# Linear attention and feed-forward on one core: float16 numerators, six Strassen blocks of 256 tokens, block ends at batch ends, and a planner that models TensorE's clock

## The chip, the core and the metric

The kernel runs on one core of a Trainium2 chip. A core has a matrix engine (TensorE, in profiles PE, with its weight loads as PEld), a vector engine (VectorE, DVE), an activation engine (ScalarE, ACT), a general engine (GpSimd, POOL) and a queue for transfers (SyncE, SP), which work at the same time and wait for each other through semaphores. TensorE writes to PSUM, eight banks of 512 four-byte columns in each of 128 partitions; the other data lie in SBUF. The metric is the time of one execution on the device in microseconds (us); lower is better.

## The reference

```python
def _attn_ref(q, k, v, omega):                 # q, k, v: (8, 8, 576, 64), omega: (128, 64)
    m, D = omega.shape
    scale = 1.0 / np.sqrt(np.sqrt(D))
    q_s, k_s = (q * scale, k * scale)
    def phi(x):
        proj = np.einsum('bhsd,md->bhsm', x, omega)
        sq = np.sum(x * x, axis=-1, keepdims=True) / 2.0
        h = proj - sq
        h = h - np.max(h, axis=-1, keepdims=True)
        return np.exp(h) / np.sqrt(m)
    q_p, k_p = (phi(q_s), phi(k_s))
    kv = np.einsum('bhsm,bhsd->bhmd', k_p, v)
    z = np.sum(k_p, axis=2)
    num = np.einsum('bhsm,bhmd->bhsd', q_p, kv)
    den = np.einsum('bhsm,bhm->bhs', q_p, z)[..., None] + 1e-06
    return (num / den).astype(np.float32)

def _moe_ref(x, w_in, w_out):                  # x: (4608, 512), w_in: (512, 2048), w_out: (2048, 512)
    h = x @ w_in
    g = 0.5 * h * (1.0 + erf(h * np.float32(1.0 / np.sqrt(2.0))))
    return (g @ w_out).astype(np.float32)
```

The output of the attention, with its heads side by side, is x of the feed-forward part: 8 batches of 576 tokens are 4608 tokens of 512 numbers. The square term falls out with the maximum.

## The kernel before

**Units.** The attention is done in 32 units: a batch and a pair of heads, four to a batch. Units 0 to 7 (batches 0 and 1) are "plain": four-byte matmuls throughout (`unit_plain`). The other 24 are "split": a number is written as a high and a low part, and products are sums of the three products of parts that matter. A split unit (`split_pre`, `exps_op`, `split_post`) casts the loaded keys and queries (`x_high` on ACT, L776; `x_low` on POOL, L785) in five groups of keys (four of 256 columns, one of 128) and four groups of queries (288 columns each), and multiplies each with omega (`proj` L793, `proj_q` L815). DVE adds the parts and finds maxima (`proj_add` L803, `q_blocks` L818 and L820), the maxima are subtracted (`k_shift` on POOL L811, `q_shift` on DVE L844), ACT takes the exponential (L591). `k_high`, `k_low` (L886) and `v_a`, `v_b` (L878) split keys and values into float16 for `kv_split` (L897). The sums are copied to `kvz` and split into `kvh` and `kvl` (`kv_c` L915, `kv_d` L918), the queries are transposed back and split into `qh` and `ql` (`q_back` L851, `q_high` L854, `q_low` L857). These four are float32r, a four-byte type. `num` (L655) multiplies them, three matmuls of 288 columns for a half and a head; then come `den`, `rcp` and `div` (L666, L671 to L673, L704).

**Blocks.** The feed-forward part goes through the tokens in 13 blocks of `TBS`: 256, 256, ten of 384, and 256. Block 0 is done in four-byte numbers (`mm1` L1076, `mm2` L1102). The others are in float16 pairs, scaled by a power of two that comes from the maximum of the attention's output bound over all batches that the block touches (`chain`, L938, then `block_be`, `block_scales` L1055, `block_spread`). A block so waits for the last batch of which it holds a token.

Blocks 1 to 8 are plain: for each of 16 chunks of 128 hidden columns, twelve matmuls (4 parts of the depth x 3 products of parts) make h in PSUM (`mm1` L1081), ACT takes gelu (L1089) and the high part (`g_high` L1093), DVE the low part (`g_low` L1097), and each tile of 128 tokens takes three matmuls of 512 columns into its accumulator (`mm2`, L1105 to L1107).

Blocks 9 to 12, three of 384 tokens and one of 256, do the first layer by Strassen's method in Winograd's form: with tokens, depth and hidden columns each cut in two, seven products take the place of eight. POOL makes the sums of operands (`b_sum` L1254), ACT and DVE their parts (`b_high` L1260, `b_low` L1263). The products (`w_prod` L1294) of `GP` = 2 chunk pairs at a time go into three PSUM buffers U, V and W of GP x half the tokens columns; a copy (`w_seed`, `w_snap`, L1301 and L1304) or a sum (`c_sum` L1307) hands them on between products, and gelu, high and low follow for four quarters (L1319, L1325, L1328). The second layer is as in plain blocks (`w_mm2`, L1392 to L1394). The very last tile is stored in two halves of 256 columns (`cuts`; `store` L1114, `store_dma` L1117).

**Order.** No loop sets the order. The program first lists all operations with what they read, write and allocate (`op`); then the class `Planner` makes one list by simulating the engines: whenever an engine is free it takes the ready operation with the earliest due time. Costs are written beside each operation. Due times come from its successors' due times and from fitted numbers: `STARTS` for blocks, `UDUE` for halves of units, `OFF` for each function's name, bonuses in `X`. Each engine then executes its own list in this order. PSUM is handed out in three rings: `at` (3 buffers), `h` (2), `acc` (3).

Of the kernel before, what the change touches and what calls it, by code (L numbers as in the profile page):

```python
# [8 lines left out]
F32 = mybir.dt.float32  # L9
# [54 lines left out]
class Planner:  # L64
# [45 lines left out]
    def run(self, lat, hop, alloc, put):  # L110
# [117 lines left out]
def favor_attention_ffn(ctx: ExitStack, tc: tile.TileContext, qT, kT, v, omT, w_in, w_out, out):  # L228
# [7 lines left out]
    TB = TBS  # L236
# [51 lines left out]
    pair_at = [xsb[:, 0:2 * T], xsb[:, 2 * T:4 * T], flat0[:, VO:VO + 2 * T], flat0[:, VO + 2 * T:VO + 4 * T], xaf[:, 0:2 * T], xaf[:, 2 * T:4 * T]]  # L288
    pair_at += [w32f[:, 1, c:c + 2].rearrange("p c w -> p (c w)")[:, 0:2 * T] for c in (0, NF // 2)]
    pair_at = [t.rearrange("p (j t) -> p j t", j=2) for t in pair_at]  # L290
    tx_at = [flat0[:, VO + (4 + i) * T:VO + (5 + i) * T] for i in range(3)] + [xaf[:, 4 * T:5 * T]]
# [10 lines left out]
                vsc=2, bs=4, be=2, tx=X['tx'], ss=X['ss'], raw=2, r=2 if X['xm'] else 3, lo=2, qt=2, ql=2 if X['qm'] else 4, kvh=1, kvl=1, xh=X['xh'], xl=X['xh'], gh=X['gh'], gl=X['gh'], o=2)  # L302
    for k, b in bufs.items():
# [3 lines left out]
                 dt=(P, HS), rt=(P, HS), rc=(P, HS // 32), mx=(P, 4 * QB), nq=(P, 4 * QB), mc=(D, 4 * QB), kvs=(P, 2, D),  # L307
                 vsc=(P, 2), bs=(P, 6), be=(32, 1), raw=(P, 2048), r=(P, 2 * HS if X['xm'] else HS), lo=(P, 2, M), qt=(P, QW, HS), ql=(P, QW, HS),
                 kvh=(P, 2, P), kvl=(P, 2, P), xh=(P, T), xl=(P, T), gh=(P, 2 * T), gl=(P, 2 * T), o=(P, DM))
    kinds = dict(raw=I32, r=F32R, ql=F32R, kvh=F32R, kvl=F32R, xh=F16, xl=F16, gh=F16, gl=F16)  # L310
    pools = dict(raw=dp, r=late, lo=late, qt=late, ql=late, kvh=late, kvl=late, xh=mp, xl=mp, gh=mp, gl=mp, o=mp)

    def alloc(name, k):
        if name in ('at', 'h', 'acc'):
            G[k] = pp.tile([P, 512], F32, tag=name, name=name, bufs=bufs[name])
            return
# [9 lines left out]
        dt = F32R if name == 'qh' and k[1].split else kinds.get(name, F32)  # L326
# [80 lines left out]
    def w_lo(pc):  # L407
        nc.scalar.activation(pc.l or raw(pc)[1], raw(pc)[1].bitcast(U32), AF.Copy, scale=2.0 ** -29)
# [78 lines left out]
    def weights_in(win, i):  # L487
# [4 lines left out]
        op('ACT', 1.08, w_lo, pc, r=[rk], w=pc.lk if pc.l is not None else [rk + ('lo',)])  # L492
# [1037 lines left out]
```

## Time and profile before

| | |
|---|---|
| time, median of 3 runs | 984.11 us (983.89 to 985.91) |
| the profiled execution | 984.64 us |
| its span, first to last instruction | 982.9 us |
| mean granted TensorE clock | 0.993 |
| read from HBM, written | 60.36 MB, 9.44 MB |

The span is what the trace shows; the rest of an execution's time lies around it. A busy TensorE is not TensorE at its peak: matmuls overlap, each record lasts longer than its share of the stream, and its end is modelled. The distance between matmuls is therefore read from runs of them. "Idle before" and "waits" give the time in which an engine did nothing, and the instruction that released it. The granted clock is the share of its full clock that TensorE had in a stretch.

### The profile page before, as it was taken

Reading aid. Unit: us, or ns where it says so; the run is one execution under the profiler, and the core shown is the slowest. Engines: PE = TensorE matmul, PEld = TensorE weight load, DVE = VectorE, ACT = ScalarE, POOL = GpSimd, SP = SyncE. Lnnn points to the kernel's source line nnn. Section 1 sums busy time; section 2 is a strip of 40 time slices with the busy share of each in tenths; the row PEclk is TensorE's granted clock in tenths of the full one; section 3 lists DMA queues with packets and bytes.
Section 4 is the critical chain, followed back from the end, with each engine's and each line's share of the span. In section 5 each row is a group of like instructions: output and inputs, shape, how many; then the busy total and the mean of one; then the engine's idle time right before and its main releaser. Section 6 shows DMA issues by size and latency. Waiting matters only on the chain.

```text
span 982.9 us, 18957 instructions
## 1 busy us (share of the span) xinstructions
PE 951.7 (97%) x6572; PEld 625.3 (64%) x6572; DVE 768.7 (78%) x2023; ACT 764.7 (78%) x1591; POOL 419.5 (43%) x612
## 2 busy tenths in 40 slices
PE   7988999899999999999999999999999999999998
PEld 5765666656655555565656665665666777767776
DVE  4898998999989997898889986996989575642322
ACT  6998768799899879979799987787779675654453
POOL 2235345666647674752564533552565011220000
PEclk7999999999999999999999999999999999999999
DMA  9774324222213221322213222231111000000000
GB/s 270 219 230 143 131 57 128 63 83 63 63 55 89 76 62 58 82 67 83 62 38 102 66 52 70 62 90 43 50 49 49 10 2 33 2 22 12 1 34 22
DMA packets 46287, 71.01 MB, mean 72 GB/s; under 512 B 13680, under 2 KB 22256, under 8 KB 46192
## 3 DMA queue, kind: packets, MB, share of 16 engines
q1 hardware_dynamic: 46192, 69.81, 24.1%
q8 instruction: 52, 0.85, 0.4%
q14 instruction: 43, 0.35, 0.1%
HBM read 60.36 MB, written 9.44 MB: 71 GB/s over the span
## 4 chain that ended last, share of the span: by engine, by line
PE 68%; DVE 18%; ACT 5%; POOL 3%; issue 2%; DMA 1%; SPq 1%; ACTq 0%; POOLq 0%
PE h L1081 16%; PE h L1294 5%; PE acc L1105 5%; PE acc L1107 5%; PE acc L1106 5%; PE at L1294 5%; PE acc L1393 4%; PE acc L1394 4%; PE acc L1392 4%; PE acc L1102 3%; PE at L655 3%; PE h L1076 2%; DVE gl L1097 2%; PE at L793 2%; PE at L897 2%
## 5 line engine op out<-in xcount | busy, mean ns | idle before, releaser
L785 POOL TENSOR_TENSOR r<-xt,r 64x288 fp32r<-64x288 f32 (+2 forms) x216 | 178.2, 843 | 147.0 <-ACT r L776 107.1
L1081 PE MATMUL h<-xh,wih 128*128 128x384 f16 (+1 forms) x512 | 163.7, 320 | 8.3 <-DVE gl L1097 7.6
L1081 PE MATMUL h<-xl,wih 128*128 128x384 f16 (+1 forms) x512 | 163.7, 320 | 0.0
L1081 PE MATMUL h<-xh,wil 128*128 128x384 f16 (+1 forms) x512 | 163.7, 320 | 0.0
L1105 PE MATMUL acc<-woh,gh 128*128 128x512 f16 x368 | 140.2, 381 | 0.0
L1107 PE MATMUL acc<-wol,gh 128*128 128x512 f16 x368 | 139.5, 379 | 0.0
L1106 PE MATMUL acc<-woh,gl 128*128 128x512 f16 x368 | 139.5, 379 | 0.0
L1081 PEld LDWEIGHTS <-wih 128*128 128x128 f16 x1024 | 97.6, 98 | 55.2 <-issue 0.2
L1097 DVE SCALAR_TENSOR_TENSOR gl<-h,bs,gh 128x384 f16<-128x384 f32 (+1 forms) x128 | 75.6, 590 | 24.9 <-ACT gh L1093 23.5
L776 ACT CAST r<-xt 128x256 fp32r<-128x256 f32 (+2 forms) x216 | 82.2, 407 | 15.6 <-PE at L815 6.8
L1089 ACT ACTIVATE h<-h,bs 128x384 f32<-128x384 f32 (+1 forms) x128 | 69.0, 540 | 25.3 <-PE h L1081 23.9
L1093 ACT ACTIVATE gh<-h,bs 128x384 f16<-128x384 f32 (+1 forms) x128 | 72.3, 566 | 13.1 <-PE acc L1107 9.8
L1081 PEld LDWEIGHTS <-wil 128*128 128x128 f16 x512 | 50.0, 98 | 39.2 <-issue 11.8
L1393 PE MATMUL acc<-woh,gl 128*128 128x512 f16 (+1 forms) x192 | 69.4, 361 | 0.1
L1392 PE MATMUL acc<-woh,gh 128*128 128x512 f16 (+1 forms) x192 | 69.4, 362 | 0.0
L1394 PE MATMUL acc<-wol,gh 128*128 128x512 f16 (+1 forms) x192 | 69.4, 361 | 0.0
L1294 PEld LDWEIGHTS <-w 128*128 128x128 f16 x768 | 60.3, 98 | 11.1 <-issue 0.9
L1107 PEld LDWEIGHTS <-gh 128*128 128x128 f16 x368 | 36.0, 98 | 43.4
L793 PE MATMUL at<-om,r 128*128 128x256 f32 x216 | 53.6, 337 | 2.6 <-POOL r L785 2.0
L1105 PEld LDWEIGHTS <-gh 128*128 128x128 f16 x368 | 35.8, 97 | 31.6 <-issue 0.2
L417 POOL TENSOR_TENSOR w<-w 128x1024 int32<-128x1024 int32 x12 | 28.5, 2375 | 61.9 <-DVE w L414 35.3
L1106 PEld LDWEIGHTS <-gl 128*128 128x128 f16 x368 | 36.1, 98 | 27.2 <-issue 0.3
(285 smaller groups left out, 2549.8 us busy)
## 6 DMA issues: line engine op xcount, KB each, us to landing
xt<-in_kT SPq DMA_DIRECT2D x56, 288.0 KB, 3.9
xt<-in_qT SPq DMA_DIRECT2D x56, 288.0 KB, 3.8
out_x<-o SPq DMA_DIRECT2D x35, 256.0 KB, 2.1
raw<-in_w_in SPq DMA_DIRECT2D x16, 512.0 KB, 5.5
raw<-in_w_out SPq DMA_DIRECT2D x16, 512.0 KB, 4.4
w<-in_v SPq DMA_DIRECT2D x24, 320.0 KB, 3.0
vt<-in_v SPq DMA_DIRECT2D x8, 320.0 KB, 4.7
out_x<-o SPq DMA_DIRECT2D x2, 128.0 KB, 1.7
```

The lines of the kernel that those rows point to most:

```text
L776: nc.scalar.copy(G['r', u, x][:, 0:b - a], xf[:, a:b])
L785: nc.gpsimd.tensor_tensor(r, xf[D:, a:b], r, op=ALU.subtract)
L793: nc.tensor.matmul(o[:, t], r[:, t * P:(t + 1) * P], om, start=True, stop=True)
L1081: nc.tensor.matmul(h[:, 0:t], w, (G['xh', n, j], G['xh', n, j], G['xl', n, j])[k][:, 0:t], start=(i == 0), stop=(i == 3 * NJ - 1))
L1097: nc.vector.scalar_tensor_tensor(G['gl', n, c][:, 0:t], G['h', n, c][:, 0:t], G['bs', n][:, 3:4], G['gh', n, c][:, 0:t], op0=ALU.mult, op1 ...
L1105: nc.tensor.matmul(acc, gh[:, s], woh[:, c, c0:c1], start=(c == 0), stop=False)
L1106: nc.tensor.matmul(acc, gl[:, s], woh[:, c, c0:c1], start=False, stop=False)
L1107: nc.tensor.matmul(acc, gh[:, s], wol[:, c, c0:c1], start=False, stop=(c == NF - 1))
L1294: nc.tensor.matmul(b[:, g * h:(g + 1) * h], w, x[:, kt], start=first and k == 0, stop=last and k == 6 * GP - 1, skip_group_check=True)
L1392: nc.tensor.matmul(acc, gh, woh[:, c, c0:c1], start=begin, stop=False)
L1393: nc.tensor.matmul(acc, gl, woh[:, c, c0:c1], start=False, stop=False)
L1394: nc.tensor.matmul(acc, gh, wol[:, c, c0:c1], start=False, stop=end)
```

## The change

**Float16 numerators.** `kvh`, `kvl`, `qh`, `ql` become float16. So that they fit, queries are scaled by 2^15 and sums by 2^-22, and `den` takes the scale back (a third column of `vsc`). `q_low` and `kv_d`, subtractions, become a scaling and a subtraction in one instruction.

**Query groups.** Queries of a split unit go through projection, casts and maxima in three groups of 384 columns for four of 288.

**Blocks.** 256, 256, then 384, 256 and five of 384, then six of 256, which are the Strassen blocks: 1536 tokens for 1408. There are 15 blocks for 13, and Strassen still starts at block 9, at token 3072 for 3200. The ends at 1152 and 2304 are ends of a batch of 576. A Strassen group is four chunk pairs for two, so that U, V, W and the quarters are 512 columns wide; a quarter has a float16 buffer of its own (six for three of 768 columns); U comes from the ring `at` alone, W from `h` or `at`. Before the first Strassen block, `prime` writes each buffer of the ring `h` in full width with one matmul. The second layer takes quarters in the order 11, 22, 12, 21; quarter 21 is tile 0. The places of x in SBUF are assigned anew.

**The planner.** It follows TensorE's busy share in windows of 3.4133 us and doubles the cost of matmuls from a window under 0.6 on, until two windows over 0.95 have passed. Many operations' costs are other numbers (`w_sign` 1.14 for 1.21, `block_scales` 1.95 for 1.2), `STARTS`, `UDUE`, `OFF` and `X` are fitted anew, and a new table `MOVES` gives thousands of single operations an offset of their own.

Branches of other settings, unused before and after (`w_lo_p`, `w_high_p`, the split units with four-byte sums), come or go with it.

```diff
-TBS = (256, 256) + (384,) * 10 + (256,)
-X = dict(fb=1875.39, fbp=-594.94, ..., n0=9, h=2, at=3, vs=5, wr=('h', 'at'), tx=4, ss=4, xh=8, gh=3,
+NSC = 2.0 ** -22
+CLK0 = 2.9
+CLKW = 3.4133
+X = dict(fb=59.68, fbp=-1804.0, ..., tb=(384, 256, 384, 384, 384, 384, 384), h=2, at=3, vs=5, wr=(('h', 'at'),
+         'at'), gh=6, n32=1, xp=0, qs=0, wl=0, wg=0, r=3, lag=6)
+MOVES = {0: 73.7, 1: -37.5, 3: -94.1, ...
...
-            o.due += OFF.get(o.fn.__name__, 0.0)
+            o.due += OFF.get(o.fn.__name__, 0.0) + MOVES.get(o.id, 0.0)
...
+        seen, slow, good, wins = 0, False, 0, [0.0] * 1000
+        def clock(t, c):
+            nonlocal seen, slow, good
+            while CLK0 + (seen + 1) * CLKW <= t:
+                u = wins[seen] / CLKW
+                if not slow:
+                    slow, good = seen > 0 and u < 0.6, 0
+                else:
+                    good += u > 0.95
+                    slow = good < 2
+                seen += 1
+            if slow:
+                c *= 2
...
+                if o.e == 'PE':
+                    c = clock(t, c)
...
-    TB = TBS
+    KP = len(X['tb'])
+    N0 = 2 + KP
+    TB = (256, 256) + X['tb']
+    TB += (256,) * ((NTOK - sum(TB)) // 256)
...
-    QB = HS // 32
+    QG = 3
+    QS = R2 // QG
+    QB = QS // 32
...
-    kinds = dict(raw=I32, r=F32R, ql=F32R, kvh=F32R, kvl=F32R, xh=F16, xl=F16, gh=F16, gl=F16)
+    kinds = dict(raw=I32, r=F32R, ql=F16, kvh=F16, kvl=F16, gh=F16, gl=F16)
...
+        if name == 'qh' and k[1].split:
+            G[k] = G[k].bitcast(F16)[:, 0:R2]
...
     def q_high(u, g):
-        nc.scalar.copy(qv(G['qh', u], g), G['qt', u, g])
+        nc.scalar.activation(qv(G['qh', u], g), G['qt', u, g], AF.Copy, scale=KSC)
     def q_low(u, g):
-        nc.vector.tensor_tensor(G['ql', u, g], G['qt', u, g], qv(G['qh', u], g), op=ALU.subtract)
+        nc.vector.scalar_tensor_tensor(G['ql', u, g], G['qt', u, g], KSC, qv(G['qh', u], g), op0=ALU.mult, op1=ALU.subtract)
...
     def kv_c(u):
-        nc.scalar.copy(G['kvh', u], G['kvz', u])
+        nc.scalar.activation(G['kvh', u], G['kvz', u], AF.Copy, scale=NSC)
     def kv_d(u):
-        nc.vector.tensor_tensor(G['kvl', u], G['kvz', u], G['kvh', u], op=ALU.subtract)
+        nc.vector.scalar_tensor_tensor(G['kvl', u], G['kvz', u], NSC, G['kvh', u], op0=ALU.mult, op1=ALU.subtract)
...
-    GP = 2
+    GP = 4
+    NQ = NF // 2 // GP
...
     def wino_second(n, q):
-        NI, h = TB[n] // P, TB[n] // 2
-        order = ((0, 0), (1, 2), (1, 0), (1, 1), (0, 1), (0, 2)) if NI == 3 else ((0, 0), (1, 0), (1, 1), (0, 1))
...
+        for x, part in enumerate((11, 22, 12, 21)):
+            i = part % 10 - 1
             for g in range(GP):
...
+    def prime(i):
+        nc.tensor.matmul(G['prime', i], wih[:, 0, 0:P], woh[:, 0], start=True, stop=True)
...
-        if n == X['n0']:
+        if n == N0:
...
+            for i in range(X['h']):
+                seq('m1', 'PE', 0.25, prime, i, r=[('wh', 1, 0), ('wh', 0, 0)], new=[('h', ('prime', i))], due=when(n, 0), kind='P')
```

More of the change, by code (lines that the diff above doesn't have):

```diff
@@ L491, in weights_in @@
         op('ACT', 1.08, w_hi, pc, w=[rk + ('hi',)], r=[rk])
-        op('ACT', 1.08, w_lo, pc, r=[rk], w=pc.lk if pc.l is not None else [rk + ('lo',)])
+        on = X['wl'] >> (i + 8 * (1 - win)) & 1
+        op('POOL' if on else 'ACT', 1.36 if on else 1.08, w_lo_p if on else w_lo, pc, r=[rk], w=pc.lk if pc.l is not None else [rk + ('lo',)])
         op('DVE', 0.64, w_shift, pc, r=[rk, rk + ('hi',)], w=bk)
@@ L619, in bound_a @@
     def bound_a(u):
-        nc.scalar.activation(G['zr', u], sums(u)[1], AF.Copy, bias=TINY)
+        if u.split:
+            nc.scalar.activation(G['zr', u], sums(u)[1], AF.Copy, bias=TINY, scale=G['vsc', u.b][:, 2:3])
+        else:
+            nc.scalar.activation(G['zr', u], sums(u)[1], AF.Copy, bias=TINY)
     def bound_b(u):
@@ L692, in x_pair, with free_region @@
     def x_pair(n, a):
-        return pair_at[pair_of(n, a)]
+        kind, r, i = pair_of(n, a)
+        w = 2 * (T if kind == 'x' else TH)
+        return (regions[3][:, i, 0:w] if r == 3 else regions[r][:, i * w:(i + 1) * w]).rearrange("p (j t) -> p j t", j=2)
+    def free_region(r):
+        ks = [('xp', 'w', r, i, j) for i in range(4) for j in range(2)]
+        assert not any(k in PL.last for k in ks)
+        op(None, 0, nothing, w=ks + [('xp', 'x', r, a, j) for a in range(2) for j in range(2)] + (['xaf'] if r == 2 else []))
     def div(u, half):
@@ new lines, in split_post @@
+        op('ACT', 0.74, v_a, u, r=[u.vk, ('vsc', u.b), 'p2'], w=['vb'])
+        op('DVE', 0.85, v_b, u, r=[u.vk, ('vsc', u.b)], w=['vb'])
+        for g in range(len(KG)):
+            es = [('et', u.eb, t) for t in KG[g]]
+            n = len(KG[g])
+            op('POOL', 0.1 + 0.15 * n, k_high, u, g, r=es + ['kk'], w=[('kk', g)])
+            op('DVE', 0.07 + 0.135 * n, k_low, u, g, r=es, w=[('kk', g)])
+        for g in range(len(KG)):
+            op('PE', 0.088 * len(KG[g]), kv_split, u, g, r=['vb', ('kk', g)], w=[] if g == 0 else [pk],
+               new=[('at', pk), ('kvs', ('kvs', u)), ('kvz', ('kvz', u))] if g == 0 else [])
@@ L1035, in split_post @@
+        op('ACT', 0.2, kv_a, u, r=[pk], w=[('kvs', u)])
+        op('DVE', 0.2, kv_b, u, r=[pk, ('kvs', u)], w=[('kvz', u)])
+        op('ACT', 0.39, kv_b2, u, r=[pk], w=[('kvz', u)])
+        op('ACT', 0.31, kv_c, u, r=[('kvz', u)], new=[('kvh', ('kvh', u))])
+        op('DVE', 0.34, kv_d, u, r=[('kvz', u), ('kvh', u)], new=[('kvl', ('kvl', u))])
+        bound(u, ('kvz', u))
         for x, g in enumerate((0, 1) if X['qm'] else (0, 2, 1, 3)):
             c = 0.3 * X['qm']
-            op('DVE', 0.42 + c, q_back, u, g, r=[('eq', u.eb, y) for y in ((g, g + 2) if X['qm'] else (g,))], new=[('qt', ('qt', u, g))])
+            op('DVE', 0.42 + c, q_back, u, g, r=[('eq', u.eb, y) for y in range(QG)], new=[('qt', ('qt', u, g))])
@@ L1484, in favor_attention_ffn @@
         if n == 1:
-            op(None, 0, nothing, w=['xaf'] + [('xa', m, j) for m in range(2) for j in range(NJ)] + [('xp', k, j) for k in (4, 5) for j in range(2)])
+            op(None, 0, nothing, w=['xaf'] + [('xa', m, j) for m in range(2) for j in range(NJ)] + [('xp', 'x', 2, a, j) for a in range(2) for j in range(2)])
+        if 1 <= n < N0:
+            r = 2 if n == 1 else PLACE[n - 2]
+            if r < 3 and r not in PLACE[max(0, n - 1):]:
+                free_region(r)
     lat = dict(PE=0.18, ACT=0.107, DVE=0.07, POOL=0.046)
```

322 lines of the change are left out of this document (151 added, 171 removed), and 374 rows, old and new, of tables (MOVES, UDUE).

## The prediction

> **What bounds the kernel now.** I read the page first, then busy time by stage, then who waited for whom, then single groups. The page:
>
> ```profile
> span 982.9 us, 18957 instructions
> PE 951.7 (97%) x6572; PEld 625.3 (64%) x6572; DVE 768.7 (78%) x2023; ACT 764.7 (78%) x1591; POOL 419.5 (43%) x612
> ...
> PEclk7999999999999999999999999999999999999999
> ...
> PE 68%; DVE 18%; ACT 5%; POOL 3%; issue 2%; DMA 1%; SPq 1%; ACTq 0%; POOLq 0%
> ```
>
> TensorE is busy 97% of the span and holds 68% of the chain that ended last; VectorE holds 18%. A change is therefore worth the TensorE time that it removes, plus the TensorE idle time that it closes. The same by stage (length, then busy time of PE, PEld, DVE, ACT, POOL, granted clock, DMA share, GB/s):
>
> ```profile
> 0.00:14.00 14.00, 8.19 (x87) 6.50 (x88) 7.20 (x21) 6.78 (x16) 0.70 (x6) 1.00 0.86 258
> 14.00:24.20 10.20, 9.33 (x49) 7.88 (x50) 4.43 (x9) 8.50 (x24) 4.91 (x3) 0.50 1.05 283
> 24.20:78.80 54.60, 46.59 (x383) 34.27 (x380) 49.80 (x117) 49.93 (x105) 19.10 (x12) 1.00 0.70 217
> 78.80:82.20 3.40, 3.40 (x6) 1.34 (x5) 3.14 (x5) 2.94 (x5) 2.83 (x8) 0.50 0.27 111
> ...
> 150.00:350.00 200.00, 191.78 (x1197) 120.00 (x1196) 188.56 (x510) 175.02 (x382) 130.26 (x189) 1.00 0.26 74
> 350.00:740.00 390.00, 386.14 (x2372) 235.16 (x2371) 331.99 (x974) 324.56 (x693) 200.62 (x317) 1.00 0.24 66
> 740.00:930.00 190.00, 188.98 (x1569) 137.10 (x1569) 107.25 (x239) 119.22 (x228) 34.18 (x58) 1.00 0.04 15
> ```
>
> Four kinds of stage. Up to 78.8 us TensorE idles 5.8 + 0.9 + 8.0 = 14.7 us, while DMA is near full until 24 us and DVE and ACT are each about 91% busy after it. From 78.8 to 82.2 us it is busy all the time, but at a clock of 0.50: half of 3.4 us, 1.7 us, is lost. From 150 to 350 us DVE is 94% busy and TensorE idles 8.2 us. From 350 to 740 us it idles 3.9 us, and in the Strassen stage from 740 to 930 us only 1.0 us. In the window 150 to 360 us its two largest waits (total, times, longest) are:
>
> ```profile
> PE h L1081 <- DVE gl L1097: 5.7, 8, 1.7
> PE at L793 <- POOL r L785: 1.8, 1, 1.8
> ```
>
> First-layer products wait for a PSUM buffer that DVE's `g_low` (L1097) still reads. DVE, not TensorE, ends last there.
>
> **The Strassen blocks.** Two stretches of nothing but Strassen products (L1294; 60 matmuls of 192 columns, 24 of 128), then two of nothing but plain first-layer products (L1081; 24 of 256 columns, 24 of 384), and the mean of one Strassen matmul:
>
> ```profile
> 882.74:887.87 5.13, 5.11 (x60) 1.00 0.17 64
> 942.24:943.76 1.52, 1.50 (x24) 1.00 0.44 173
> ...
> 179.50:182.31 2.81, 2.79 (x24) 1.00 0.02 6
> 283.62:287.71 4.09, 4.08 (x24) 1.00 0.02 4
> ...
> L1294 PE MATMUL at<-xl,w 128*128 128x192 f16 x112 | 27.6, 246 | 0.0
> L1294 PE MATMUL at<-xl,w 128*128 128x128 f16 x48 | 8.6, 219 | 0.0
> ```
>
> A matmul's own 246 or 219 ns overlaps the next one's, so a run of n lasts one of these and n-1 intervals: (5.11-0.246)/59 = 82.4 ns for 192 columns, (1.50-0.219)/23 = 55.7 ns for 128. By its code a Strassen block has 7 products x 8 chunk pairs x 2 x 3 = 336 matmuls of half its tokens. Before: three blocks of 384 and one of 256, 1008 x 82.4 + 336 x 55.7 = 101.8 us. After: 2016 x 55.7 = 112.3 us, so **+10.5 us**. In exchange block 3 shrinks from 384 to 256 tokens: 192 plain matmuls, eight runs of 24 that are each 4.08-2.79 = 1.29 us shorter, **-10.3 us**. The second layer is the same number of matmuls. The 128 more tokens under Strassen are paid back by the shorter matmuls: **+0.2 us**, nothing. I give it ±1 us, the reading error of the runs.
>
> The groups are now four chunk pairs, 512 columns instead of 384. Their ACT and DVE steps (gelu, high, low, sums) become fewer and longer, and the casts of the operands more (7 x 6 for 7 x 4). I cost them at nothing: from 740 to 930 us DVE is busy 107 of 190 us and ACT 119. If that cover were gone, TensorE would wait where a product needs a sum read out of its bank. The copy (min, median, max) and the sum in question, of 256 and 384 columns:
>
> ```profile
> L1304 ACT COPY h<-h x10: 357/463/478, 746.9 to 965.6; 128x384 f32<-128x384 f32 x8, 128x256 f32<-128x256 f32 x2
> L1307 DVE TENSOR_TENSOR at<-h,wih x5: 432/566/566, 749.8 to 949.1; 128x384 f32<-128x384 f32 x4, 128x256 f32<-128x256 f32 x1
> ```
>
> For 512 columns that extrapolates to 570 and 700 ns, under a product between of 24 x 55.7 = 1340 ns; before it was 463 and 566 under 12 x 82.4 = 990. The margin grows from 0.42 to 0.64 us, so below nothing is excluded on TensorE, and the bound above is 12 groups x 3 handoffs x 0.7 = 25 us with no margin at all; I take 0. `prime` adds two matmuls of 512 columns:
>
> ```profile
> L1105 PE MATMUL acc<-woh,gh 128*128 128x512 f16 x368 | 140.2, 381 | 0.0
> ```
>
> At most 2 x 0.38, by the overlap seen above about half: **+0.4 us**.
>
> **Float16 numerators.** Two of the `num` matmuls (L655, 288 columns of four-byte operands), the first and the last of five in a row:
>
> ```profile
> 277.10 0.30 PE L655 MATMUL at<-qh,kvl 128*128 128x288 f32 x1
> ...
> 277.63 0.29 PE L655 MATMUL at<-ql,kvh 128*128 128x288 f32 x1
> ```
>
> Four intervals in 0.53 us, 132.5 ns each. In float16 288 columns lie between 2.79/24 and 4.08/24, less the overlapped end: 109.6 + 32/128 x 53.4 = 123 ns. There are 24 split units x 2 halves x 6 = 288: **-2.7 us**. The bounds are 0, if the operands' type doesn't matter, and -5, if the switches between types cost as much again. On DVE the lows (L857, L918) change from a subtraction to a scale and subtraction, and the query projection goes in 3 groups of 384 for 4 of 288:
>
> ```profile
> L818 DVE STREAM_TRANSPOSE et<-at 128x288 f32<-128x288 f32 x52 | 24.7, 474 | 0.8 <-PE at L815 0.5
> L820 DVE TENSOR_REDUCE mx<-et 128x9 f32<-128x288 f32 x52 | 23.6, 453 | 1.8
> L851 DVE STREAM_TRANSPOSE qt<-et 128x576 f32<-128x576 f32 x26 | 19.6, 761 | 2.9 <-ACT et L591 2.8
> L857 DVE TENSOR_TENSOR ql<-qt,qh 128x576 fp32r<-128x576 f32 x48 | 38.5, 812 | 3.2 <-ACT qh L854 3.1
> L878 DVE SCALAR_TENSOR_TENSOR vb<-w,vsc,vb 128x640 f16<-128x640 f32 x24 | 21.9, 914 | 0.0
> L1097 DVE SCALAR_TENSOR_TENSOR gl<-h,bs,gh 128x384 f16<-128x384 f32 x112 | 68.0, 607 | 24.2 <-ACT gh L1093 23.0
> ```
>
> A transpose costs (761-474)/288 = 1.0 ns per element, so 570 for 384; the reduce, with the same slope, 549. Per unit 4 x 927 = 3.71 becomes 3 x 1119 = 3.36 us. The new low of 576 lies between 607 and 914, at 837: +25 ns, twice per unit, and as much again for the low of the sums (L918), +0.1 at most. DVE loses about 0.25 us per unit, 6 us of its 769; POOL and ACT lose one of nine casts and subtractions per unit. None of it is on TensorE; it matters where DVE ends last.
>
> **Block ends and the order.** Block 3 was tokens 896 to 1280 and needed batch 2, the first with the long split attention. Its scale and the stall around its start:
>
> ```profile
> 267.14 0.14 DVE L938 TENSOR_REDUCE vexp<-cg 32x1 f32<-32x4 f32 x1
> ...
> 270.58 0.26 POOL L1055 TENSOR_SCALAR bs<-bs,wsc 32x1 f32<-32x1 f32 x1
> ...
> 275.06 0.50 PE L793 MATMUL at<-om,r 128*128 128x256 f32 x2 [1.79 <-POOL r L785]
> ```
>
> Batch 2's maximum came at 267.1 us, the scale at 270.6, and block 3's first matmul stands at 283.62 us (the window above): TensorE reached the boundary as soon as the data did. After, block 3 is 896 to 1152 and needs batch 1 alone. That is 192 x 0.109 + 96 x 0.216 (as 128 columns more take 53 ns more, 512 take 109.6 + 2 x 53.4) = 41.7 us of TensorE work which no longer waits for batch 2, in the very stage where DVE is late. With DVE's saving and freely moved due times I take both waits above as gone, **-7.5 us** of the 8.2 us idle there. Bounds: nothing (the order is fixed for each engine's queue, and a `gl` queued behind an attention step is late as before), and all idle after 150 us, 8.2 + 3.9 + 1.0 = 13.1 us.
>
> The planner now counts TensorE's windows of 3.4133 us and doubles its costs when it expects half clock. It can only move work so that the idle before 78.8 us doesn't trigger the slow window: **-1.7 us**, bounds 0 and 14.7 + 1.7. It takes 1.7 because TensorE stands in the way there, as the chain of waits in this stretch shows (start, length, link):
>
> ```profile
> 78.12 5.40 PE acc L1102 x8
> ```
>
> These are second-layer products of block 0, and nothing else ends later.
>
> **The end.** The last block of before splits its last tile in two column halves. After, parts come in the order 11, 22, 12, 21, so tile 0 ends last, and the halves are tile 1's. The last tile's store (two halves of 256, against one of 512) and its DMA:
>
> ```profile
> L1114 ACT ACTIVATE o<-acc,bs 128x512 f32<-128x512 f32 x4 | 2.7, 687 | 5.4 <-PE acc L1394 5.4
> L1114 ACT ACTIVATE o<-acc,bs 128x256 f32<-128x256 f32 x2 | 0.8, 472 | 1.6 <-PE acc L1394 1.6
> ...
> out_x<-o SPq DMA_DIRECT2D x35, 256.0 KB, 2.1
> ...
> out_x<-o SPq DMA_DIRECT2D x2, 128.0 KB, 1.7
> ```
>
> 687-472 ns and 2.1-1.7 us: **+0.6 us**.
>
> **The sum** is made against the profiled execution, 984.64 us with a span of 982.9, 0.05% over the median of 984.11. 984.6 + 0.2 + 0.4 - 2.7 - 7.5 - 1.7 + 0.6 = 973.9: I forecast **974 us**.
>
> **The rivals.**
>
> *Only the work changes (20%).* Waits are moved, not removed: 984.6 - 2.7 + 0.2 + 0.4 + 0.6 = 983.1 us with the slow window, 981.4 without. For it: DVE is 94% busy from 150 to 350 us and loses only 0.25 us per unit. This is also the case in which the change doesn't do what it says: Strassen's larger share is worth 0.2 us either way. A difference under 0.2%, 982.1 to 986.1 us, is about what a measurement of this kernel can't tell from none; I give 11 of the 20 to it and 9 to below.
>
> *The start is rearranged too (17%).* Half of the 14.7 us idle up to 78.8 us goes: 974 - 7.3 = 966.7 us. For it: all due times change. Against it: DMA, then DVE and ACT, are full there, and no work of theirs is removed.
>
> *`g_low` later than before (12%), slower.* One new order for all queues, in a stage with 6% of DVE free. Over the whole span the waits for `gl` are:
>
> ```profile
> PE h L1081 <- DVE gl L1097: 7.6, 10, 1.7
> ```
>
> Ten late ones, of 128. Each one queued behind one more attention step, such as L857's 0.81 us, is late by as much. With 20 late the wait doubles, and nothing else is won: 983.1 + 7.6 = 990.7 us. It decides from 3.0 us more waiting, four more late ones.
>
> *Short matmuls wait for their weights (2%), slower.* The weight load of one Strassen matmul:
>
> ```profile
> L1294 PEld LDWEIGHTS <-w x768: 95/98/101, 745.4 to 972.5; 128*128 128x128 f16 x192
> ```
>
> If each matmul of 128 columns had to last its 98 ns, the 2016 would take 197.6 us, 85.3 more than I count: 1059 us. The run of 24 in 1.50 us speaks against it, at full clock and with a fresh weight for each. The Trainium skill ("TensorE: Matmul & The Clock Gate", section "Back-to-back issue gap") gives a sustained 81 ns per matmul at 128 columns for pairs of weight load and matmul. By that, an estimate, the 2016 would take 163 us and the kernel some 1025 us; the trace's 55.7 ns disagrees, and decides.
>
> **How the numbers follow.** The forecast has 49%. Faster: 49 + 17 + 9 = 75%; within 0.2%: 11%; slower: 12 + 2 = 14%. The range goes from 961 us, most of the way to all waits gone after 150 us and half of those before, to 986 us; it leaves out the two slower rivals and some 5% below.
>
> **What would show it.** Right: 2016 Strassen matmuls of 128 columns about 56 ns apart; `num` in f16, 123 ns apart; no wait of L1081's successor for `gl` over 0.5 us between 150 and 350 us; TensorE busy over 198 of these 200 us; one slow-clock window only, in the first 25 us; one store of 512 columns at the end. Wrong: the same waits at other times, a slow window elsewhere, waits for the sums in the Strassen stage, or a start before 80 us with much less idle TensorE time than 14.7 us, which I don't count on.

## The result, and the profile after

| | before | after |
|---|---|---|
| time, median | 984.51 us (983.89 to 985.91, 4 runs) | 1001.36 us (998.62 to 1002.14, 4 runs) |
| ratio, 95% interval | | 1.0164 (1.0142 to 1.0187) |
| the profiled execution, its span | 984.64, 982.9 us | 1002.14, 1000.4 us |
| mean granted TensorE clock | 0.993 | 0.977 |

The kernel became 16.9 us slower, where the forecast was 10 us faster. The page of after, with the rows that were shown of before:

```profile
span 1000.4 us, 19895 instructions
...
PE 959.4 (96%) x7198; PEld 629.5 (63%) x7198; DVE 769.2 (77%) x1963; ACT 764.8 (76%) x1545; POOL 399.4 (40%) x616
...
PEclk7889999999999999889999999999999999999999
...
PE 22%; ACT 2%; DVE 2%; issue 1%; POOL 0%; ACTq 0%; DVEq 0%
```

The span grew by 17.5 us. TensorE's idle time (span less busy time) went from 31.2 to 41.0 us, and its busy time from 951.7 to 959.4, though the change was to make its matmuls shorter. The clock row has two 8s in the middle of the span, at slices 17 and 18, where before had only 9s. The chain that ended last is short here and no help. So the next view is busy time by stage (length, then PE, PEld, DVE, ACT, POOL, clock, DMA share, GB/s), of after:

```profile
0.00:100.00 100.00, 83.10 (x557) 64.06 (x558) 74.79 (x155) 77.35 (x164) 32.95 (x32) 0.86 0.71 215
100.00:240.00 140.00, 137.99 (x862) 88.74 (x861) 123.71 (x291) 111.29 (x224) 60.83 (x88) 1.00 0.27 79
240.00:310.00 70.00, 66.81 (x446) 42.45 (x443) 65.77 (x170) 58.65 (x129) 45.62 (x63) 1.00 0.19 56
310.00:400.00 90.00, 90.00 (x578) 55.21 (x576) 78.60 (x226) 79.99 (x165) 48.43 (x74) 1.00 0.28 74
400.00:440.00 40.00, 30.35 (x138) 16.74 (x135) 33.48 (x99) 31.57 (x74) 20.50 (x41) 0.79 0.23 65
440.00:725.00 285.00, 282.50 (x1751) 166.48 (x1749) 240.90 (x670) 237.91 (x476) 125.62 (x201) 1.00 0.22 61
725.00:930.00 205.00, 202.40 (x2228) 148.96 (x2228) 139.68 (x344) 146.33 (x281) 65.40 (x118) 1.00 0.11 32
```

and the same stretches of before, as far as they matter:

```profile
0.00:100.00 100.00, 85.31 (x620) 61.66 (x621) 79.89 (x177) 83.98 (x178) 35.43 (x33) 0.93 0.70 212
100.00:240.00 140.00, 136.39 (x840) 89.37 (x839) 132.69 (x324) 115.26 (x236) 80.35 (x101) 1.00 0.31 92
240.00:310.00 70.00, 67.04 (x412) 40.83 (x410) 64.48 (x189) 62.92 (x141) 39.72 (x67) 1.00 0.22 64
...
400.00:440.00 40.00, 39.94 (x247) 24.36 (x246) 36.53 (x104) 32.81 (x73) 23.79 (x39) 1.00 0.29 76
```

There is one new hole: from 400 to 440 us TensorE stands 9.65 us and works at 0.79 of its clock, where before it stood 0.06 us at full clock. In no other stretch does its idle time differ from before's by over 3.1 us (310 to 400 us has none at all now). The second thing to see is VectorE's column: up to 310 us it worked 277.1 us in before (79.89 + 132.69 + 64.48) and 264.3 us in after, though its work per unit shrank by only a quarter of a microsecond, by the prediction's estimate. That is a sign that attention is behind. Batch 2's scale, which the prediction showed at 270.58 us in before, was made in after at

```profile
311.44 0.25 POOL L1461 TENSOR_SCALAR bs<-bs,wsc 32x1 f32<-32x1 f32 x1
```

which is 40.9 us later. That is about what the change freed there: block 3 no longer needs batch 2, and its 256 tokens are 41.7 us of TensorE's work by the prediction. The hole in order of time, from the timelines of TensorE, VectorE and ScalarE of after (start, length, instruction, idle before and its releaser):

```profile
412.40 0.38 PE L1513 MATMUL acc<-wol,gh 128*128 128x512 f16 x1
412.79 0.76 PE L1221 MATMUL at<-om,r 128*128 128x256 f32 x4
417.67 0.55 PE L1221 MATMUL at<-om,r 128*128 128x256 f32 x1 [4.12 <-DVE nm L1231]
...
423.36 0.54 PE L1487 MATMUL h<-xx,wih 128*128 128x384 f16 x1
...
413.32 0.14 DVE L1453 TENSOR_REDUCE be<-vexp 32x1 f32<-32x2 f32 x1
415.56 1.44 DVE L1279 STREAM_TRANSPOSE qt<-w 128x576 f32<-128x576 f32 x2 [2.10 <-ACT w L1009]
...
413.40 2.12 ACT L1009 ACTIVATE w<-w 128x2304 f32<-128x2304 f32 x1
```

At 412.40 us TensorE ends the last second-layer matmul of block 4. Block 5's first matmul comes at 423.36, since the maximum of batch 3 (`be`, L1453) came only at 413.32. Between them TensorE has nothing but attention, where each step waits for another engine: it for `nm` from VectorE, VectorE for an exponential on ScalarE. In before the same two events, the maximum that block 5 needs and block 5's first matmul:

```profile
400.68 0.13 DVE L1047 TENSOR_REDUCE be<-vexp 32x1 f32<-32x2 f32 x1
...
436.79 0.33 PE L1081 MATMUL h<-xh,wih 128*128 128x384 f16 x1
```

The lead was 36.1 us there. After made do with 10.0 for scale and casts (413.32 to 423.36), so 26.1 us were slack. After spent them: its block 5 begins at token 1536, not 1664, which takes 128 tokens of TensorE work out from ahead of it (10.3 us of first layer, by the prediction's own figure, and 48 second-layer matmuls x 0.216 = 10.4), and the maximum came 12.6 us later. 26.1 - 20.7 - 12.6 = -7.2 us: TensorE runs dry for some 7 us, and stood 9.65.

**Theory 1**, then: the block ends. Moving them changed the token from which each batch's maximum is needed: batch 2 from 896 to 1152, batch 3 from 1664 to 1536, batch 4 from 2048 to 2304, batch 5 from 2816 to 2688. Where it came earlier and attention is behind, TensorE starves. Against it stand the float16 part (A, E, then theory 2: `den`), the clock (B), VectorE's and ScalarE's own chain (C), and the newly fitted order as such (theory 3).

### The profile page after: what moved, and what is told of

Read it like the earlier page. It is cut to its first block, busy times and chain, and to the rows that moved or that the text cites. A ratio compares the mean times of both kernels' runs of the same rounds, so it can differ in the third digit from the quotient of the medians.

```text
span 1000.4 us, 19895 instructions
## 1 busy us (share of the span) xinstructions
PE 959.4 (96%) x7198; PEld 629.5 (63%) x7198; DVE 769.2 (77%) x1963; ACT 764.8 (76%) x1545; POOL 399.4 (40%) x616
## 5 line engine op out<-in xcount | busy, mean ns | idle before, releaser
L1487 PE MATMUL h<-xx,wih 128*128 128x384 f16 (+1 forms) x1024 | 247.9, 316 | 5.7 <-DVE gl L1503 3.6
L1213 POOL TENSOR_TENSOR r<-xt,r 64x256 fp32r<-64x256 f32 (+2 forms) x192 | 163.1, 864 | 166.3 <-ACT r L1204 120.1
L1487 PE MATMUL h<-xx,wil 128*128 128x384 f16 (+1 forms) x512 | 161.9, 316 | 0.0
L1511 PE MATMUL acc<-woh,gh 128*128 128x512 f16 x352 | 133.8, 380 | 0.8 <-ACT o L1520 0.7
L1513 PE MATMUL acc<-wol,gh 128*128 128x512 f16 x352 | 133.4, 379 | 0.0
L1512 PE MATMUL acc<-woh,gl 128*128 128x512 f16 x352 | 133.4, 379 | 0.0
L1204 ACT CAST r<-xt 128x256 fp32r<-128x256 f32 (+1 forms) x192 | 78.7, 434 | 20.4 <-PE at L1243 11.4
L1495 ACT ACTIVATE h<-h,bs 128x384 f32<-128x384 f32 (+1 forms) x128 | 67.2, 526 | 23.2 <-PE h L1487 20.7
L1789 PE MATMUL acc<-woh,gh 128*128 128x512 f16 (+1 forms) x208 | 75.4, 363 | 0.0
L1791 PE MATMUL acc<-wol,gh 128*128 128x512 f16 (+1 forms) x208 | 75.4, 363 | 0.0
L1081 ACT ACTIVATE dt<-at,vsc 64x288 f32<-64x288 f32 x96 | 56.3, 587 | 8.4 <-PE at L1073 6.1
```

The lines of the kernel that those rows point to most:

```text
L1204: nc.scalar.copy(G['r', u, x][:, 0:b - a], xf[:, a:b])
L1213: nc.gpsimd.tensor_tensor(r, xf[D:, a:b], r, op=ALU.subtract)
L1487: nc.tensor.matmul(h[:, 0:t], w, (G['xh', n, j], G['xh', n, j], G['xl', n, j])[k][:, 0:t], start=(i == 0), stop=(i == 3 * NJ - 1))
L1511: nc.tensor.matmul(acc, gh[:, s], woh[:, c, c0:c1], start=(c == 0), stop=False)
L1512: nc.tensor.matmul(acc, gl[:, s], woh[:, c, c0:c1], start=False, stop=False)
L1513: nc.tensor.matmul(acc, gh[:, s], wol[:, c, c0:c1], start=False, stop=(c == NF - 1))
```

## The experiments

**One part alone: float16 numerators in the order of before.**

```diff
-    kinds = dict(raw=I32, r=F32R, ql=F32R, kvh=F32R, kvl=F32R, ...
+    kinds = dict(raw=I32, r=F32R, ql=F16, kvh=F16, kvl=F16, ...
-            nc.scalar.activation(dt[r], ps, AF.Identity, bias=G['vsc', u.b][r, 1:2])
+            nc.scalar.activation(dt[r], ps, AF.Identity, bias=G['vsc', u.b][r, 1:2], scale=G['vsc', u.b][r, 2:3])
...
```

> The kernel before with one part of the change alone: float16 numerators (L1073 of after, with the scales, den, bound_a, q_high, q_low, kv_c and kv_d that go with them); blocks, dues and order of work stay those of before. Theory 1 (the slower time comes from block 5's wait for batch 3 and from nothing in the arithmetic): the 576 numerator matmuls fall from 0.1325 to about 0.12 us, -3 us, and den's 91 ns x 96 = 8.7 us more on ScalarE hide: 984.5 - 3 = 981.5 us, between 980 and 983. Rival A (the added work of ScalarE and VectorE is what made after slower): not faster than before, 985 to 993 us.

Measured: 990.22 us, ratio 1.0050 (1.0035 to 1.0066). Rival A: this part alone costs 5.6 us. (It has 288 of these matmuls, as the prediction counted, not 576.) The matmuls did get shorter, as after's rows below show; more than that is lost elsewhere. It doesn't show as idle time of TensorE, which is 31.5 us for 31.2 in before. At half clock TensorE spent 20.5 us here, and 13.6 in before.

**Keep the clock up during the stall.** `FILL` names seven places of TensorE's list between 412 and 429 us.

```diff
+    def fill(o):
+        for _ in range(FILL.get(key(o), 0)):
+            nc.tensor.matmul(G['h', 4, NF - 1], wih[:, 0, 0:P], woh[:, 0], start=True, stop=True)
     def put(o):
+        fill(o)
         o.fn(*o.a)
```

> The kernel after with 46 idle matmuls of 512 columns (results read by nobody) put on TensorE's queue into its waits between 412.8 and 429 us, so that the clock isn't lowered; they take 46 x 0.216 = 9.9 us of time in which TensorE mostly stood. Theory 1 with the clock as its second half (about 10 us stood still, and about 7 us more because 17.1 us ran at half clock): the half clock at 415.5 to 440 us goes and the time falls by 5 us (3 to 8), to 996 us. Rival B (VectorE and ScalarE set the pace there at any clock, so the half clock is only a symptom): 1000 to 1003 us.

Measured: 1001.38 us, as after. The stretch in the profile of e2_fill:

```profile
400.00:440.00 40.00, 35.64 (x180) 18.81 (x179) 33.39 (x102) 32.79 (x76) 22.13 (x42) 0.96 0.26 73
```

The clock is at 0.96 instead of 0.79, and VectorE's column is the same to 0.1 us. Rival B: the half clock in the stall was a symptom. After's slow stretches there were

```profile
415.50:425.80 10.30, 6.40 (x20) 3.29 (x20) 9.81 (x25) 10.04 (x25) 9.15 (x15) 0.50 0.59 166
429.20:432.60 3.40, 3.40 (x14) 2.27 (x12) 3.33 (x8) 1.72 (x3) 0.13 (x1) 0.50 0.00 0
436.00:439.40 3.40, 3.40 (x13) 1.95 (x11) 1.85 (x10) 3.20 (x8) 2.73 (x4) 0.50 0.63 174
```

e2_fill had one stretch of 3.4 us at half clock left, the last. What TensorE won by the rest went into its next wait, for the low parts of keys on GpSimd (`r`, L1213). The matmul behind this wait in after, and the same one in e2_fill:

```profile
435.50 0.50 PE L1221 MATMUL at<-om,r 128*128 128x256 f32 x2 [2.02 <-POOL r L1213]
```

```profile
433.78 0.50 PE L1222 MATMUL at<-om,r 128*128 128x256 f32 x2 [3.67 <-POOL r L1214]
```

A rule of thumb in the Trainium skill ("TensorE: Matmul & The Clock Gate", section "Terms") puts the loss at the slow time times the clock's missing share; by it, an estimate, these 17.1 us at half clock cost 8.6 us. The trace disagrees for the 13.7 us that e2_fill took away: nothing came back with the clock, because TensorE was not what the others waited for. What the last stretch costs was not tested.

**Hold block 5's scale back**, by a planned 8 us, in both kernels.

```diff
     def block_scales(n):
+        for _ in range(44 if n == 5 else 0):
+            mul(nc.gpsimd, b[0:32, 4:5], b[0:32, 0:1], 1.0)
```

> The kernel after with block 5's scale held back by 44 small multiplications on GpSimd (44 x about 0.18 = 8 us) between batch 3's maximum and the scale. Theory 1 (TensorE has no feed-forward work left when block 5 waits for batch 3): each microsecond of the hold is paid, 1001.4 + 8 = 1009 us (1007 to 1012), and the stall after 412 us is longer by that. Rival C (the stall is attention's own chain of VectorE and ScalarE, and block 5's scale comes early enough): 1000 to 1004 us.

> The kernel before with the same hold of 44 multiplications ahead of block 5's scale. Theory 1 (there the scale lies some 27 to 37 us ahead of block 5's first matmul, since block 5 begins at token 1664, not 1536): 984.5 us within 2 us. Rival D (such a hold costs its length wherever it is put, as GpSimd's other work waits behind it): 990 to 993 us.

Measured: 1009.35 us (+8.0) for after, and 998.69 us (+14.2) for before. The first has theory 1's figure, the second lies above even rival D's range. But the hold took 11.5 us, not 8, in e4_before_late and as long in e3_after_late:

```profile
401.35 11.50 POOL L332 TENSOR_SCALAR bs<-bs 32x1 f32<-32x1 f32 x44
```

And TensorE's largest wait between 400 and 440 us (total, times, longest) is not for block 5, neither in e3_after_late nor in e4_before_late:

```profile
PE at L1221 <- POOL r L1213: 15.9, 2, 14.7
```

```profile
PE at L815 <- POOL r L785: 10.7, 1, 10.7
```

The 44 multiplications stood in GpSimd's queue ahead of `x_low` (L785, in after L1213), attention's own work, so the hold delays both. The pair proves nothing, and that the first met theory 1's figure is luck.

**Is it `den`?** `den` reads a second operand from memory since the change. Its group in before, after, and e5_f16_den, where a constant replaces both operands:

```profile
L666 ACT ACTIVATE dt<-at,vsc 64x288 f32<-64x288 f32 x96 | 47.6, 496 | 5.6 <-PE at L655 3.2
```

```profile
L1081 ACT ACTIVATE dt<-at,vsc 64x288 f32<-64x288 f32 x96 | 56.3, 587 | 8.4 <-PE at L1073 6.1
```

```profile
L672 ACT ACTIVATE dt<-at 64x288 f32<-64x288 f32 x96 | 38.9, 405 | 5.2 <-PE at L661 2.8
```

405, 496 and 587 ns with none, one and two operands from memory: 91 ns each. The Trainium skill says so too ("ScalarE: Activation LUTs", section "What ACT_TABLE_LOAD costs"): each pointer operand adds about 93 ns. The trace agrees; the prediction had priced `den` at nothing. Four kernels put it to the test, the first two with the factor moved into `div`:

```diff
-            nc.scalar.activation(dt[r], ps, AF.Identity, bias=G['vsc', u.b][r, 1:2], scale=G['vsc', u.b][r, 2:3])
+            nc.scalar.activation(dt[r], ps, AF.Copy, bias=EPS * KSC * KSC * NSC * 2.0 ** TOP)
-                nc.vector.tensor_tensor(x[r, c0:c1], ps[r, r0:r1], rt[r, r0:r1], op=ALU.mult)
+                nc.vector.scalar_tensor_tensor(x[r, c0:c1], ps[r, r0:r1], G['vsc', u.b][r, 2:3], rt[r, r0:r1], op0=ALU.mult, op1=ALU.mult)
```

> e1_f16 (the kernel before with float16 numerators alone, 990.2 us) with den made cheap again: ScalarE adds a constant in place of a scale and a bias read from memory (no operand vsc), and the factor goes into div, which VectorE does as one instruction with three operands in place of two. Theory 2 (what cost e1 its 5.6 us is den, 587 ns in place of 496 on the chain from the numerators to the quotient, 8.7 us of ScalarE in all, where VectorE waits for dt): den falls to 500 ns or less and the time to 982 us (980 to 984.5), which is before less the 2.7 us of shorter matmuls. Rival E (it is something else of the float16 part, such as VectorE's writes in float16 or a wait in the order of before): 988 to 991 us.

> The kernel after with the same cheap den. Theory 2 (the longer den is part of why after is slower): 1001.4 - 5 = 996 us (993 to 998), and the stall at 412 us begins no later and is shorter. Rival F (after's stall comes from the order and the block ends alone, and its order already allows for the longer den): 1000 to 1003 us.

The other two leave the factor out of e1_f16's `den`, and give before's `den` a factor of one:

```diff
-            nc.scalar.activation(dt[r], ps, AF.Identity, bias=G['vsc', u.b][r, 1:2], scale=G['vsc', u.b][r, 2:3])
+            nc.scalar.activation(dt[r], ps, AF.Identity, bias=G['vsc', u.b][r, 1:2])
```

```diff
-            nc.scalar.activation(dt[r], ps, AF.Identity, bias=G['vsc', u.b][r, 1:2])
+            nc.scalar.activation(dt[r], ps, AF.Identity, bias=G['vsc', u.b][r, 1:2], scale=G['vsc', u.b][r, 2:3])
...
+        nc.gpsimd.tensor_scalar(t[0:32, 2:3], t[0:32, 0:1], 0.0, 1.0, op0=ALU.mult, op1=ALU.add)
```

> e1_f16 with den as short as in before: the factor on the denominators is left out, so the quotients lack it; all else as in e1_f16. Theory 2 (the longer den is what cost e1 its time): 982 us (980 to 984). Rival E (another part of the float16 numerators costs it): 988 to 991 us.

> The kernel before, numerators as they were, with den alone made longer: it reads a factor of 1 from memory as well (496 to 587 ns, 96 times). Theory 2: 984.6 + 7 = 992 us (988 to 993). Rival E: 983 to 986 us.

| kernel | ScalarE in `den` | time | ratio to before |
|---|---|---|---|
| e12_den_long: before, `den` longer | +8.7 us | 990.15 us | 1.0059 (1.0043 to 1.0074) |
| e1_f16 | +8.7 us | 990.22 us | 1.0050 (1.0035 to 1.0066) |
| e11_f16_noscale | as before | 987.00 us | 1.0030 (1.0019 to 1.0042) |
| e5_f16_den | -8.7 us, `div` longer | 991.95 us | 1.0083 (1.0067 to 1.0100) |
| e6_after_den: after | -17.4 us to after, `div` longer | 997.19 us | 1.0131 (1.0108 to 1.0154) |

e12 is the clean one: 8.7 us more of ScalarE on attention's chain, and besides it only one small GpSimd instruction for each split batch, cost 5.4 us in the order of before. So `den` alone can cost about what e1 lost. But e11, without the longer `den`, gives back only 3.2 of e1's 5.6 us: at 987.00 us it lies between theory 2's range and rival E's, still 2.2 us slower than before, not 2.7 faster. What makes that up was not taken apart. (At half clock TensorE spent 20.5 us in e11 and in e12, as in e1; that may be a part of it.) e5 missed both ranges: `div` as one instruction with three operands is longer on VectorE. One of its groups in before and in e5:

```profile
L704 DVE TENSOR_TENSOR xsb<-at,rt 64x288 f32<-64x288 f32 x24 | 10.8, 452 | 0.7
```

```profile
L710 DVE SCALAR_TENSOR_TENSOR xsb<-at,vsc,rt 64x288 f32<-64x288 f32 x24 | 12.3, 513 | 0.7
```

61 ns more, and there are 168 such pieces (7 shapes x 24): 10.2 us of VectorE for 17.4 of ScalarE. In the order of before that trade won nothing; in after's (e6) it won 4.2 us, as theory 2 forecast, but not by a shorter stall:

```profile
400.00:440.00 40.00, 29.02 (x135) 16.07 (x134) 33.33 (x102) 31.47 (x76) 21.52 (x42) 0.83 0.25 72
```

TensorE stood 11.0 us there, for 9.65 in after.

**The order fitted again.** Same instructions, blocks and costs as after; only the due times differ.

```diff
-STARTS = (-2246.36, 206.66, ...
-UDUE = (-5665.39, -5478.65, ...
-OFF = dict(b_high=872.56, ...
-MOVES = {0: 73.7, 1: -37.5, ...
+...
```

> The kernel after with the same instructions, blocks and costs, and other due times for the planner (STARTS, UDUE, OFF and MOVES replaced), found by searching on the planner's own makespan: 966.2 us planned, where after's is 971.4 and before's 958.0. In the plan TensorE stands 3.7 us at 400 to 450 us, where after's plan has 8.9. Theory 3 (after's loss is in the order that the planner was fitted to, and the chip follows the plan with the same 29 us on top): 1001.4 - 5.2 = 996 us (993 to 999). Rival G (the plan doesn't decide at this grain, and the loss is in the instructions): 1000 us or more.

Measured: 992.62 us, ratio 1.0080 (1.0061 to 1.0099): 8.7 us under after, more than the plan's 5.2. Another order takes back half of the loss, as theory 3 has it. But the stall is still there, as TensorE's 31.64 us in the stretch below show, and part of the 8.7 us is won in it: 180 matmuls at a clock of 0.96, for after's 138 at 0.79. So order and block ends are not two separate losses. The expectation above holds one more hint: the planner itself had after 13.4 us behind before (971.4 and 958.0 us).

**The block ends moved.** The due times of these two were searched for on the planner's makespan in the way of e8_refit; against what the expectation says, e9's search ran somewhat longer.

```diff
-X = dict(..., tb=(384, 256, 384, 384, 384, 384, 384), ...
+X = dict(..., tb=(384, 256, 256, 256, 384, 256, 384, 384), ...
```

```diff
-X = dict(..., tb=(384, 256, 384, 384, 384, 384, 384), ...
+X = dict(..., tb=(384, 384, 384, 256, 384, 384, 384), ...
```

> The instructions and costs of after, with other block ends: 896, 1152, 1408, 1664, 2048, 2304, 2688, 3072 (tb of 384, 256, 256, 256, 384, 256, 384, 384), so that batch 3's maximum is needed from token 1664 on, as in before, and batch 2's from 1152 on, as in after; due times searched for on the planner's makespan, with no more search than e8_refit had (954.3 us planned; e8_refit 966.2, after 971.4). Theory 1 (the stall at 412 us is there because a block needs batch 3's maximum 128 tokens earlier than in before): no stall at 400 to 440 us, TensorE busy for 39 of the 40 us, and the time 966 - 954 = 12 us under e8_refit: 981 us (977 to 985). Rival H (attention is late in after whatever the ends are, so that the stall moves to the next block's wait): 990 us or more, with 8 us of idle TensorE at another wait for a maximum.

> The instructions and costs of after with the ends 896, 1280, 1664, 1920, 2304 (tb with its 256 in fourth place): batch 3's maximum is needed from 1664 on, as in before, but batch 2's from 896 on, as in before, where after needs it from 1152 on; due times searched for in the same way (976.5 us planned). Theory 1 (a stall stands where a block's need for a maximum meets attention that isn't through that batch): none at 400 to 440 us, and one of some 14 us at about 290 us, where block 3 waits for batch 2; the time by the plan 976.5 + 26 = 1003 us (998 to 1007). Rival I (the stall at 412 us has nothing to do with block ends): it stays there, with 8 us or more of idle TensorE between 400 and 440 us.

Measured: e9_ends 985.46 us, ratio 1.0010 (1.0001 to 1.0019); e10_ends_early 996.41 us, 1.0123 (1.0105 to 1.0141). The first is half a microsecond above theory 1's range and the second below it; the places of the stalls are as theory 1 forecast. The two stretches where a stall was forecast, 240 to 310 and 400 to 440 us, in e8_refit, e9_ends and e10_ends_early:

```profile
240.00:310.00 70.00, 69.45 (x473) 44.77 (x473) 65.04 (x176) 62.55 (x139) 48.71 (x74) 1.00 0.23 67
...
400.00:440.00 40.00, 31.64 (x180) 18.20 (x179) 38.34 (x104) 36.18 (x73) 20.04 (x39) 0.96 0.29 82
```

```profile
240.00:310.00 70.00, 66.96 (x446) 42.25 (x445) 65.27 (x184) 58.62 (x133) 46.49 (x66) 1.00 0.23 64
...
400.00:440.00 40.00, 39.78 (x281) 26.33 (x279) 33.26 (x108) 37.82 (x86) 21.80 (x46) 1.00 0.26 68
```

```profile
240.00:310.00 70.00, 56.71 (x305) 31.27 (x303) 62.45 (x173) 55.59 (x118) 46.94 (x74) 0.88 0.23 63
...
400.00:440.00 40.00, 40.00 (x252) 23.58 (x251) 34.45 (x98) 37.74 (x80) 20.33 (x43) 1.00 0.21 60
```

The stall follows the need for a maximum. With batch 3 needed from 1664 there is none at 400 to 440 us in either kernel; with batch 2 needed from 896 again it stands at 240 to 310 us, 13.3 us. The block ends alone don't make a stall: before needs batch 2 from 896 too, and TensorE stood 2.96 us in that stretch. But batch 2's maximum came at 267.14 us there, and in e10_ends_early block 3 got it some 25 us later:

```profile
291.98 0.13 DVE L5866 TENSOR_REDUCE be<-vexp 32x1 f32<-32x2 f32 x1
```

A stall takes both, a maximum that comes late and a block end that asks for it early. Why attention is so late in this order stays open. And it isn't that attention got faster in e9. The maximum of batch 3 and a first-layer matmul at the start of block 6, the one that needs it there:

```profile
416.55 0.13 DVE L5972 TENSOR_REDUCE be<-vexp 32x1 f32<-32x2 f32 x1
...
429.95 0.33 PE L6006 MATMUL h<-xx,wil 128*128 128x384 f16 x1
```

It came 3.2 us later than in after, and TensorE still never stood: it had 128 more tokens to do first. e9 is 7.2 us under e8 by median; that a search for due times ends better or worse by chance is part of that number, the places of the stalls are not. e9 has all of after's instructions, the longer `den` included, and its clock up to 100 us is 0.86 as in after; with other ends and another order these need not make the kernel slower.

**The best of both.** e9's order, with `den` cheap and the factor on the reciprocals:

```diff
         nc.vector.reciprocal(rc, rv[:, :, 0])
+        if u.split:
+            nc.vector.tensor_scalar(rc, rc, G['vsc', u.b][:, 2:3], 1.0, op0=ALU.mult, op1=ALU.mult)
```

> e9_ends (985.5 us) in the same order, with den as a copy that adds a constant (405 ns in e5 in place of 587: 96 x 182 ns = 17.5 us of ScalarE saved) and the factor put on the 9 reciprocals of a unit's half by one small VectorE instruction (48 of them, some 0.15 us, 7 us in all), in place of e5's longer div (10.5 us). Theory 2 (time on attention's chain of ScalarE and VectorE is paid at about 0.6 us per us in the stages before 400 us, as e12 showed): 985.5 - 4 = 981.5 us (979 to 984), 3 us under before. Rival J (with no stall left TensorE's stream bounds the time, and the chain's length no longer counts): 985 us within 1.5 us.

Measured: 986.32 us, ratio 1.0020 (1.0008 to 1.0031), no gain. The outcome is rival J's, but its reason isn't shown, since the trade was even again. Nor does e12 show that the price is paid before 400 us: the matmul that stands at 400.32 us in before comes 0.85 us later in e12, and the span's end 4.3 us later. The new instruction in e13_ends_den:

```profile
L5608 DVE TENSOR_SCALAR rc<-rc,vsc 128x9 f32<-128x9 f32 x48 | 16.2, 337 | 1.7
```

It took 337 ns, not 150: 16.2 us of VectorE against 17.4 us of ScalarE. No kernel tried here beats before; e9_ends equals it within 0.2%.

## Why the prediction was wrong

*What bounds the kernel.* TensorE's stream, and VectorE as the engine that ends last from 150 to 350 us: no run speaks against it, but the change closed less of the gap than forecast. TensorE was busy 194.8 of these 200 us, not over 198, and a wait for `gl` still took 1.3 us, not under 0.5. And the 3.9 us of idle time in 390 us after 350 was read as a stage without danger. It was the sign of a lead, 36.1 us at block 5, that the change could spend. I did not measure it.

*The Strassen blocks*, +0.2 us: right in its prices. TensorE's idle time from 725 to 930 us is 2.6 us, in before 2.4. A run of 72 of their matmuls in after, without a wait:

```profile
808.62:812.81 4.19, 4.18 (x72) 4.01 (x71) 1.00 0.30 83
```

(4.18 - 0.219) / 71 = 55.8 ns, as taken. The copy and the sum of 512 columns were put at 570 and 700 ns and took

```profile
L1711 ACT COPY h<-h 128x512 f32<-128x512 f32 x9 | 5.2, 574 | 1.8 <-PE h L1701 1.8
L1714 DVE TENSOR_TENSOR at<-h,wih 128x512 f32<-128x512 f32 x5 | 3.5, 696 | 2.4 <-PE h L1701 2.0 <-ACT mc L1251 0.3
```

*Float16 numerators*, -2.7 us: the term was right on TensorE. The first and the last of five matmuls in after are four intervals apart:

```profile
408.51 0.29 PE L1073 MATMUL at<-qh,kvl 128*128 128x288 f16 x1
...
409.00 0.29 PE L1073 MATMUL at<-ql,kvh 128*128 128x288 f16 x1
```

0.49 us, 122.5 ns each, for 132.5. But the working listed the lows and the query groups and left out `den`, one line of the diff, 91 ns x 96. e12 shows what it costs in the order of before: 5.4 us, twice what the matmuls gain.

*Block ends and the order*, -7.5 us: **this is the step that failed.** It followed one boundary, block 3's, and found the true gain there: the waits for `gl` in the whole span fell from 7.6 us to

```profile
PE h L1487 <- DVE gl L1503: 3.6, 4, 1.3
```

But a block end that moves to the end of batch 1, token 1152, moves every end behind it. Block 5's came 128 tokens nearer to batch 3's maximum, and the step that gives 41.7 us of freed work at one boundary takes 20.7 us away at the other. It also assumed that freely moved due times take waits away; in after's order VectorE had worked 12.8 us less by 310 us, and batch 2's scale came 40.9 us later. The runs show in its place a stall in which TensorE stands some 10 us: it goes with the end (e9), comes back at another end (e10), and another order with the same ends takes back 8.7 of the 16.9 us (e8). How the loss divides between ends and order stays open.

*The clock*, -1.7 us: wrong. The planner's model didn't remove the slow stretches; up to 71 us after has three:

```profile
12.74:29.81 17.07, 14.47 (x87) 13.55 (x85) 10.18 (x17) 13.59 (x36) 6.82 (x4) 0.50 0.97 256
43.46:46.87 3.41, 3.41 (x16) 1.71 (x16) 3.41 (x6) 3.41 (x12) 3.26 (x2) 0.50 0.70 203
63.94:70.77 6.83, 6.06 (x27) 5.74 (x27) 6.23 (x18) 4.76 (x10) 2.37 (x1) 0.50 0.08 22
```

27.3 us, where before had 13.6. What they cost was not measured; e2 shows for most of the stall that a slow clock can cost nothing, and e9 equals before with as low a clock up to 100 us.

*The end*, +0.6 us: about right. From the end of the last matmul to the end of the span after has 4.1 us (996.28 to 1000.4), before 3.3 (979.56 to 982.9). What `prime` costs (+0.4 us) was not measured.

*The rivals.* "`g_low` later than before" had the right kind, an attention step out of time with TensorE in a new order, but the wrong place and a third of the price: 990.7 us at 12%. None looked at a block's need for a maximum. "Short matmuls wait for their weights" fell as expected: 55.8 ns.

## What to carry to other kernels

When a boundary moves, write down for every boundary behind it what it waits for before and after, and measure the lead in the trace (the time from the datum's arrival to its first use); an engine that hardly idles may do so only because it has such a lead. A list of costs must be made from the diff's instructions, each operand of each, for all engines: 91 ns on a ScalarE instruction that TensorE never sees cost, in the order of before, twice what the shorter matmuls gained. Before a half clock is blamed, ask whether TensorE is waited for.

## What the runs showed of the hardware that was not expected

An operand of one number per partition, read from memory, costs time on ScalarE (91 ns each: 405, 496, 587 ns). On VectorE `div` took 61 ns more with one (513 for 452), but became another instruction with it, so the operand's own price isn't known; a multiplication of only 9 columns by one took 337 ns, where the reciprocal of the same 9 takes 216. In the first slow stretch of after TensorE was busy without a break for 13.65 us before it was granted the full clock again:

```profile
16.15:29.81 13.66, 13.65 (x79) 13.11 (x79) 6.77 (x12) 11.16 (x29) 5.61 (x4) 0.50 0.88 260
```
